# A gated scan and a dense layer on one core: value and state products of both chunks in one visit, the state added in place, four tiles for the gate's split parts

## The chip, the core and the metric

The kernel runs on one core of one Trainium2 chip. The metric is the device time of one execution in microseconds. A profile is one execution recorded by the hardware profiler; its span runs from the first to the last instruction of the program.

The engines are named as in the profile: PE is TensorE (matmuls), PEld its weight loads, DVE is VectorE, ACT is ScalarE, POOL is GpSimd, SP is SyncE, which here only issues DMAs.

## The reference

```python
# all inputs of the scan: (4, 8, 768, 48): batch, head, time, width
mag = sqrt(a_re**2 + a_im**2)
a = (a_re + 1j * a_im) * minimum(mag, 0.999) / (mag + 1e-6)
S = 0                                          # per batch and head, 48 x 48
for t in range(768):
    S = a[t][:, None] * S + outer(k[t], v[t])
    y[t] = q[t] @ S.real
x = y as (3072, 384)                           # 8 heads x 48 side by side
h = x @ w_in                                   # 384 -> 2048
g = h where h >= 1, 0 where h <= -1, else (h + 1)**2 / 4
out = g @ w_out                                # 2048 -> 384
```

So there are two parts: a linear recurrence with a complex decay for each column of the keys, and a dense layer with a piecewise gate.

## The kernel before, in words

**Units and blocks.** The 4 x 768 tokens are cut into 12 units of 256 tokens, and a unit into two chunks of 128. A batch has three units, called parts 0, 1 and 2; units of two batches take turns. Two units form a block of 512 tokens, and there are six blocks. The dense layer works on blocks, the scan on units.

**The scan without a loop over time.** `gates(u)` (L569) makes, on ScalarE and VectorE, running sums of the logarithm and the angle of the decay, multiplies them into keys and queries as a real and an imaginary part, and moves the results by DMA into tiles `hd`, with the 96 rows of a head side by side. What is left is done by `attend(u)` (L898) with matmuls in fp32:

- `scores(c)` (L979): for the eight heads in two groups of four, keys times queries of a chunk, 128 x 128 each, into a bank of PSUM (`sc`, L989). VectorE multiplies by a triangle on the way out (`am`, L997).
- `transposes(c)` (L924): the keys of a chunk, turned, in two groups of four heads (`tp`, L933); ScalarE copies each group out (`kT`, L939).
- `products(c)` (L950): turned keys times values, the chunk's addition to the state (`dp`, L962). VectorE adds it to the old state, into the other one of two tiles of the batch (`st`, L974).
- `values(c, ...)` (L1011): the output of a chunk, for each pair of heads the state times the queries (`yp`, L1030) and then the masked scores times the values (L1038), gathered in one bank. ScalarE copies it to `xr` (L1050), and after the second chunk six DMAs move rows within `xr` (L1062).

`values` and `products` use 64 columns of the array at a time, with two heads side by side; the other matmuls use 96 or 128.

**Banks.** From the third unit on all these outputs take turns over three banks of PSUM, `at0` to `at2`, in the order in which the Python code makes the tiles (`bank`, L917). The other five hold two tiles of gate inputs (`h0`, `h1`) and three of outputs (`o0` to `o2`).

**The dense layer.** `moe(blk)` (L1145) splits x into a high and a low part (fp32r), and does each product in three matmuls. For each of 16 slices f of 128 columns: `gemm1(f)`, nine matmuls in groups of three (`h`, L1160); the gate, on ScalarE and VectorE (`s` L1185, `g` L1204 and L1212, or for the first `SPARE` blocks two more passes on ScalarE, L1195 and L1199, in place of L1212); its split into a high part by a ScalarE cast (`gh`, L1218) and a low one by VectorE (`gl`, L1222); and `gemm2(f)`, nine matmuls in groups of three (`o`, L1235). `gh` and `gl` take turns over six tiles, so three slices can be under way.

**What sets the order.** The code first lists all operations with an estimated cost, what they read and write, and for some a due time. `Plan.order` (L169) then plays them through engine by engine: an engine that is free takes, of the operations that are ready, the one with the earliest due time. The program is emitted in that order, and each engine runs its own list in order on the chip. Three details matter:

- What a tile has to wait for is worked out from the tile that was *made* before it on the same slot, and from those of its operations that are listed already (L155 and L156).
- Parts of a *visit* are glued (L1077): when one is placed, the next is placed right behind it, if all that it waits for has been placed by then (L271); if not, it is taken up later like any other. A gate or output group of three matmuls can then come between.
- An attention visit's due time lies in a window of the block before (`WINDOW`, `EARLY`), spread evenly over the unit's visits (L1109).

The planner's estimates, in ns: PE to another engine 260, ScalarE or VectorE to another 190 (`LAT`); a ScalarE copy from PSUM 80 + 0.77 a column, a VectorE operation 66 + 1.04 a column; `products` 8 x 124, times 0.92 in a visit.

A unit's visits before: scores of chunk 0; transposes of chunk 0; values and products of chunk 0 with half the scores of chunk 1; the other half with the transposes of chunk 1; values and products of chunk 1. In part 2 the last transposes and products fall away.

**Start and end.** Until about 70 us units 0 and 1 and the weights are prepared; PE runs filler matmuls (`idle`, L1290) in the gaps. After the last block some checks of the inputs' ranges follow.

Of the kernel before, what the change touches and what calls it, by code (L numbers as in the profile page):

```python
# [10 lines left out]
F32 = mybir.dt.float32  # L11
# [7 lines left out]
P = 128  # L19
NB = 4  # L20
NH = 8
# [23 lines left out]
LATER = 4  # L45
SUM = 1.0e6
# [18 lines left out]
LATE_MOVE = 1000  # L65
# [7 lines left out]
QUEUE = (2, 0.0)  # L73
WINDOW = (0.0, 0.7)
EARLY = (0.15, 1.05)
HEAD = ((15000, 8000), (8000, 2000))
HOME = 4
SPARE = 2
# [243 lines left out]
def gated_scan_moe(  # L322
# [11 lines left out]
    sums = const.tile([P, 2, P], F32, name="sums")  # L334
    mask = sums[:, 0]
    make_upper_triangular(nc, mask)
    nc.gpsimd.memset(sums[:, 1], 1.0)
# [9 lines left out]
    keys = [const.tile([P, 4 * HR + 32], F32, name=f"kT{g}") for g in range(2)]  # L347
# [32 lines left out]
    def turn_of(tag, n):  # L380
        k = seen.get(tag, 0)
        seen[tag] = k + 1
        return f"{tag}{k % n}"
# [514 lines left out]
    def attend(u):  # L898
# [25 lines left out]
        def transposes(c):  # L924
            cs = slice(c * CH, (c + 1) * CH)
            out = []
            for g in range(2):
                TP = bank([P, 4, HR], f"tp_{u}_{g}_{c}")
                KT = pl.tile(f"kT{g}", lambda g=g: keys[g])

                def run(g=g, TP=TP):
                    for i, h in enumerate(GROUPS[g]):
                        PE_.transpose(TP.get()[:, i, :], head(h)[:, 0, cs], ident[:HR, :HR])  # L933

                def tail(TP=TP, KT=KT):
                    pl.op(
                        "ACT",
                        act(4 * HR, psum=True),
                        lambda: A_.copy(  # L939
                            KT.get()[:, : 4 * HR].rearrange("p (h r) -> p h r", h=4), TP.get()  # L940
                        ),
                        r=[TP],
                        w=[KT],
                    )

                out.append((4 * 83, run, [hd[h // 3] for h in GROUPS[g]], TP, tail))
                carry.setdefault("kT", []).append(KT)
            return out

        def products(c):  # L950
            kT = carry.pop("kT")
            DP = bank([P, NH, D], f"dp_{u}_{c}")
            V_c = carry["V"]
            old = carry.get(b)
            ST = tl(turn_of(f"st{b % 2}", 2), [HR, NH, D], F32, f"st_{u}_{c}")
            carry[b] = ST

            def run():
                for i in range(NH):
                    for a in (0, 64):  # L960
                        k = HR * (i % 4) + a
                        PE_.matmul(  # L962
                            DP.get()[a : a + 64, i, :],
                            kT[i // 4].get()[:, k : k + 64],
                            V_c[0].get()[:, V_c[1], i * D : (i + 1) * D],
                            start=True,
                            stop=True,
                        )

            def tail():  # L970
                if old is None:
                    fn = lambda: V_.tensor_copy(ST.get(), DP.get()[:HR])
                else:
                    fn = lambda: V_.tensor_tensor(ST.get(), old.get(), DP.get()[:HR], op=ALU.add)  # L974
                pl.op("DVE", dve(DM), fn, r=[DP] + ([old] if old else []), w=[ST])

            return [(NH * 124, run, [*kT, V_c[0]], DP, tail)]
# [33 lines left out]
        def values(c, ams, st):  # L1011
# [5 lines left out]
            def part(prs):  # L1017
                Y = bank([P, len(prs), CH], f"yp_{u}_{c}_{prs[0]}")

                def run():  # L1020
                    for i, pr in enumerate(prs):
                        for kind in (0, 1):
                            if kind == 0 and st is None:
                                continue
                            for e in range(2):
# [3 lines left out]
                                if kind == 0:  # L1029
# [4 lines left out]
                                        start=True,  # L1034
                                        stop=False,
                                    )
                                else:
# [4 lines left out]
                                        start=st is None,  # L1042
                                        stop=True,
# [16 lines left out]
                return ((4 if st else 2) * len(prs) * 110 + (400 if prs[0] == 0 else 0), run, r, Y, tail)  # L1060
# [29 lines left out]
        if part == 0:  # L1090
            carry.pop("kT", None)
        state_after = lambda c: part * NC + c < S // CH - 1
        for c in range(NC):
# [9 lines left out]
            pending = (ams, carry.get(b))  # L1103
            carry["V"] = (V, c)
        last = values(NC - 1, *pending)
        if state_after(NC - 1):
            last = last + products(NC - 1)
        visit(last)
# [36 lines left out]
    def moe(blk):  # L1145
# [7 lines left out]
        def gemm1(f):  # L1153
# [25 lines left out]
            GH = tl(turn_of("gg", 6), [P, T], F32R, f"gh_{blk}_{f}")  # L1179
            GL = tl(turn_of("gg", 6), [P, T], F32R, f"gl_{blk}_{f}")  # L1180
# [399 lines left out]
```

## Time and profile before

| | us |
|---|---|
| median of three runs | 577.53 (577.27 to 579.56) |
| the profiled execution | 577.35 |
| its span | 575.6 |
| first gate matmul (`h`) | 70.41 |
| last output matmuls (`o`) begin, 27 in a row | 562.16 |
| PE busy in the span | 561.4 |
| DVE busy | 434.5 |
| ACT busy | 406.1 |
| mean granted clock of TensorE | 0.998 |

In the rows below, `L989` is a line of the kernel, `sc<-hd` is what is written and what is read, and `x8` counts instructions; one matmul in fp32 is two of them, but for transposes. In a timeline a row is a stretch of like instructions: its start, its length, engine, line, and in brackets how long the engine stood idle before it and what it waited for. A group's row gives the busy time, the mean in ns of one, and the idle time before them.

### The profile page before, as it was taken

Reading aid. Unit: us, or ns where it says so; the run is one execution under the profiler, and the core shown is the slowest. Engines: PE = TensorE matmul, PEld = TensorE weight load, DVE = VectorE, ACT = ScalarE, POOL = GpSimd, SP = SyncE. Lnnn points to the kernel's source line nnn. Section 1 sums busy time; section 2 is a strip of 40 time slices with the busy share of each in tenths; the row PEclk is TensorE's granted clock in tenths of the full one; section 3 lists DMA queues with packets and bytes.
Section 4 is the critical chain, followed back from the end, with each engine's and each line's share of the span. In section 5 each row is a group of like instructions: output and inputs, shape, how many; then the busy total and the mean of one; then the engine's idle time right before and its main releaser. Section 6 shows DMA issues by size and latency. Waiting matters only on the chain.

```text
span 575.6 us, 9984 instructions
## 1 busy us (share of the span) xinstructions
PE 561.4 (98%) x3922; PEld 478.4 (83%) x3922; DVE 434.5 (75%) x625; ACT 406.1 (71%) x654; POOL 1.7 (0%) x20
## 2 busy tenths in 40 slices
PE   8999999999999999999999999999999999999995
PEld 7798978888888888888888888888888888888883
DVE  4999999999979498579589878887885544455452
ACT  7776799887998998975576666667643333369972
POOL 1000000000000000000000000000000000000000
PEclk9999999999999999999999999999999999999999
DMA  8676571773641614712601613402312200078811
GB/s 352 250 198 192 163 262 55 192 282 114 188 173 48 195 68 125 237 57 82 174 2 52 202 56 102 153 2 85 114 56 72 74 1 7 21 265 309 298 42 61
DMA packets 23527, 77.42 MB, mean 134 GB/s; under 512 B 4528, under 2 KB 10288, under 8 KB 23472
## 3 DMA queue, kind: packets, MB, share of 16 engines
q1 hardware_dynamic: 23472, 76.70, 40.8%
q8 instruction: 33, 0.54, 0.4%
q14 instruction: 22, 0.18, 0.1%
HBM read 51.90 MB, written 4.72 MB: 98 GB/s over the span
## 4 chain that ended last, share of the span: by engine, by line
PE 78%; DVE 12%; ACT 5%; DMA 2%; issue 1%; SPq 0%; ACTq 0%; DVEq 0%
PE o L1235 30%; PE h L1160 29%; PE sc L989 6%; PE yp L1038 3%; PE yp L1030 3%; PE dp L962 2%; PE tp L933 1%; PE idle L1290 1%; ACT ai L608 1%; DVE kq L725 1%; DMA xr<-xr 1%; DMA ai<-in_art_dram 1%; DVE g L1204 1%; ACT x L608 1%; DVE raw_i L440 1%
## 5 line engine op out<-in xcount | busy, mean ns | idle before, releaser
L1160 PE MATMUL h<-xH,wi 128*128 128x512 f32 x576 | 180.6, 395 | 1.2 <-DVE g L1204 0.9
L1235 PE MATMUL o<-gh,wo 128*128 128x512 f32 x576 | 180.4, 394 | 0.0
L1160 PEld LDWEIGHTS h<-xH,wi 128*128 128x128 f32 x576 | 106.2, 188 | 22.6 <-DVE g L1204 1.1
L1235 PEld LDWEIGHTS o<-gh,wo 128*128 128x128 f32 x576 | 106.3, 188 | 21.6 <-issue 0.7
L1204 DVE TENSOR_TENSOR g<-h,s 128x512 f32<-128x512 f32 x96 | 65.9, 687 | 63.1 <-ACT s L1185 45.6
L1160 PE MATMUL h<-xL,wi 128*128 128x512 f32 x288 | 112.6, 391 | 0.0
L1235 PE MATMUL o<-gl,wo 128*128 128x512 f32 x288 | 112.5, 391 | 0.0
L1185 ACT ACTIVATE s<-h,cst 128x512 f32<-128x512 f32 x96 | 65.7, 685 | 42.0 <-PE h L1160 38.9
L1218 ACT CAST gh<-g 128x512 fp32r<-128x512 f32 x96 | 59.1, 616 | 46.0 <-DVE g L1212 43.6
L1222 DVE TENSOR_TENSOR gl<-g,gh 128x512 fp32r<-128x512 f32 x96 | 66.0, 687 | 31.9 <-ACT gh L1218 31.8
L1160 PEld LDWEIGHTS h<-xL,wi 128*128 128x128 f32 x288 | 54.1, 188 | 12.1 <-DVE xL L1137 0.4
L1235 PEld LDWEIGHTS o<-gl,wo 128*128 128x128 f32 x288 | 54.1, 188 | 11.6
L608 ACT ACTIVATE ai<-ai 128x768 f32<-128x768 f32 x49 | 41.2, 843 | 19.1 <-DVE ai L777 8.6
L989 PE MATMUL sc<-hd 96*128 96x128 f32 x384 | 49.6, 278 | 0.0
L989 PEld LDWEIGHTS sc<-hd 96*128 96x128 f32 x384 | 47.0, 192 | 2.2
L1212 DVE SCALAR_TENSOR_TENSOR g<-s,g 128x512 f32<-128x512 f32 x64 | 44.2, 691 | 1.8
L1038 PE MATMUL yp<-am,V 128*64 128x128 f32 x384 | 35.5, 273 | 0.2 <-DVE am L997 0.2
L997 DVE TENSOR_TENSOR am<-sc,sums 128x512 f32<-128x512 f32 x48 | 32.5, 683 | 3.1 <-PE sc L989 2.8
L1290 PE MATMUL idle<-sums,ident 128*128 128x128 f32 x238 | 31.3, 291 | 1.7 <-POOL sums masks.py:66 1.7
L1030 PE MATMUL yp<-hd,st 96*64 96x128 f32 x320 | 32.1, 278 | 0.3 <-DVE am L997 0.3
L1290 PEld LDWEIGHTS idle<-sums,ident 128*128 128x128 f32 x238 | 30.3, 206 | 2.5 <-POOL sums masks.py:66 1.7
L402 ACT ACT_TABLE_LOAD x21 | 26.9, 1283 | 0.4
(104 smaller groups left out, 651.6 us busy)
## 6 DMA issues: line engine op xcount, KB each, us to landing
chk<-in_wl_dram SPq DMA_DIRECT2D x16, 768.0 KB, 5.2
kq<-in_kq_dram SPq DMA_DIRECT2D x12, 768.0 KB, 4.7
ai<-in_ari_dram SPq DMA_DIRECT2D x10, 768.0 KB, 6.1
hd<-x SPq DMA_DIRECT2D x24, 288.0 KB, 4.1
hd<-kq SPq DMA_DIRECT2D x24, 288.0 KB, 4.9
raw_i<-in_wl_dram SPq DMA_DIRECT2D x8, 768.0 KB, 4.6
raw_o<-in_wl_dram SPq DMA_DIRECT2D x8, 768.0 KB, 5.8
V<-in_v_dram SPq DMA_DIRECT2D x12, 384.0 KB, 3.2
```

The costliest lines, as they stand in the source:

```text
L608: lambda: A_.activation(out(), src(), f, **kw),
L989: PE_.matmul(SC.get()[:, i, :], t[:, 0, cs], t[:, 1, cs], start=True, stop=True)
L1030: PE_.matmul(o_, st.get().rearrange("p h e -> p (h e)")[:, lo : lo + 64], head(h)[:, 1, cs], start=True, stop=False,)
L1038: PE_.matmul(o_, V.get()[:, c, lo : lo + 64], ams[pr // 2].get()[:, 2 * (pr % 2) + e, :], start=st is None, stop=True,)
L1160: PE_.matmul(H.get(), weight["i", f // 2].get()[:, f % 2, part, sl], x.get()[:, j, :], start=j == 0 and n == 0, stop=j == NJ - 1 and n == 2,)
L1185: lambda: A_.activation(SS.get(), H.get(), AF.Relu, bias=c_half, scale=-0.5 if spare else 0.5),
L1204: lambda: V_.tensor_tensor(G.get(), H.get(), SS.get(), op=ALU.max),
L1212: lambda: V_.scalar_tensor_tensor(G.get(), SS.get(), 1.0, G.get(), op0=ALU.min, op1=ALU.mult),
L1218: pl.op("ACT", act(T), lambda: A_.copy(GH.get(), G.get()), r=[G], w=[GH])
L1222: lambda: V_.tensor_tensor(GL.get(), G.get(), GH.get().bitcast(F32), op=ALU.subtract),
L1235: PE_.matmul(PO[m].get(), weight["o", f // 2].get()[:, f % 2, part, sl], g.get(), start=f == 0 and n == 0, stop=f == NF - 1 and n == 2,)
L1290: PE_.matmul(idle["h1"], ident, mask, start=True, stop=True)
```

## The change

It has these parts:

- From unit 2 on (`JOINED`) a unit's visits are: scores of chunk 0 with half of its transposes; the other half with the scores of chunk 1; the transposes of chunk 1; values and products of both chunks. In the last visit the products of chunk 1 stand ahead of the values of chunk 1, and their addition to the state is listed after the values. The tiles of both chunks' scores and transposes are made before any visit is listed.
- For that, two more tiles of masked scores (`am2`, `am3`) and two more of turned keys (`kT2`, `kT3`).
- The state of a batch is one tile, and the products are added in place. For each pair of heads the masked scores' product now comes ahead of the state's.
- `gh` and `gl` take turns over four tiles, and the code lists `gemm2` one slice after `gemm1` where it listed it three after; due times are the same.
- The triangle for the running sums lies in the space of `am3` and is made apart from the mask.
- `SPARE` goes from 2 to 1: the second block's gate uses the VectorE operation (L1212). `HOME`, `WINDOW`, `EARLY`, `QUEUE` and `LATE_MOVE` change: which tiles the first weights land in, the windows of the visits, when SyncE holds back a DMA for a more urgent one, and 1000 ns of allowance for a move that falls away.

```diff
+JOINED = 2
-LATE_MOVE = 1000
+LATE_MOVE = 0
-QUEUE = (2, 0.0)
-WINDOW = (0.0, 0.7)
-EARLY = (0.15, 1.05)
+QUEUE = (2, 10000.0)
+WINDOW = (0.3, 0.7)
+EARLY = (0.6, 0.7)
-HOME = 4
-SPARE = 2
+HOME = 6
+SPARE = 1
...
-    sums = const.tile([P, 2, P], F32, name="sums")
-    mask = sums[:, 0]
+    mask = const.tile([P, P], F32, name="mask")
     make_upper_triangular(nc, mask)
+    sums = sb.tile([P, 4, CH], F32, tag="am3", name="sums", bufs=1)[:, :2]
+    make_upper_triangular(nc, sums[:, 0])
...
-                KT = pl.tile(f"kT{g}", lambda g=g: keys[g])
+                k = g + 2 * (c % 2 if u >= JOINED else 0)
+                KT = pl.tile(f"kT{k}", lambda k=k: keys[k])
...
-            old = carry.get(b)
-            ST = tl(turn_of(f"st{b % 2}", 2), [HR, NH, D], F32, f"st_{u}_{c}")
-            carry[b] = ST
+            first = b not in carry
+            if first:
+                carry[b] = tl(f"st{b % 2}", [HR, NH, D], F32, f"st_{b}")
+            ST = carry[b]
...
-                    fn = lambda: V_.tensor_tensor(ST.get(), old.get(), DP.get()[:HR], op=ALU.add)
+                    fn = lambda: V_.tensor_tensor(ST.get(), ST.get(), DP.get()[:HR], op=ALU.add)
...
-                AM = tl(f"am{g}", [P, 4, CH], F32, f"am_{u}_{g}_{c}")
+                k = g + 2 * c if u >= JOINED else g
+                AM = tl(f"am{k}", [P, 4, CH], F32, f"am_{u}_{g}_{c}")
...
-                        for kind in (0, 1):
+                        for kind in (1, 0):
...
+        if u >= JOINED:
+            (sc0, am0), (sc1, am1) = scores(0), scores(1)
+            tp0 = transposes(0)
+            tp1 = transposes(1) if state_after(1) else []
+            visit(sc0 + tp0[:1])
+            visit(tp0[1:] + sc1)
+            if tp1:
+                visit(tp1)
+            st = state_of()
+            both = values(0, am0, st) + products(0)
+            st = state_of()
+            last = values(1, am1, st, 0)
+            if tp1:
+                ((*dp, add),) = products(1)
+                *head_, (*yp, copy) = last
+                last = [(*dp, lambda: None), *head_, (*yp, lambda: (copy(), add()))]
+            visit(both + last)
+        for c in range(NC) if u < JOINED else ():
...
-            GH = tl(turn_of("gg", 6), [P, T], F32R, f"gh_{blk}_{f}")
-            GL = tl(turn_of("gg", 6), [P, T], F32R, f"gl_{blk}_{f}")
+            GH = tl(turn_of("gg", 4), [P, T], F32R, f"gh_{blk}_{f}")
+            GL = tl(turn_of("gg", 4), [P, T], F32R, f"gl_{blk}_{f}")
...
-        for k in range(NF + LAG):
+        for k in range(NF + 1):
             if k < NF:
                 gemm1(k)
-            if k >= LAG:
-                gemm2(k - LAG)
+            if k:
+                gemm2(k - 1)
```

More of the change, by code (lines that the diff above doesn't have):

```diff
@@ L345, in gated_scan_moe @@
     ones = c_one
-    keys = [const.tile([P, 4 * HR + 32], F32, name=f"kT{g}") for g in range(2)]
+    keys = [const.tile([P, 4 * HR + 32], F32, name=f"kT{g}") for g in range(4)]
     for t in keys:
@@ L946, in transposes @@
                 out.append((4 * 83, run, [hd[h // 3] for h in GROUPS[g]], TP, tail))
-                carry.setdefault("kT", []).append(KT)
+                carry.setdefault(("kT", c), []).append(KT)
             return out
         def products(c):
-            kT = carry.pop("kT")
+            kT = carry.pop(("kT", c))
             DP = bank([P, NH, D], f"dp_{u}_{c}")
-            V_c = carry["V"]
-            old = carry.get(b)
-            ST = tl(turn_of(f"st{b % 2}", 2), [HR, NH, D], F32, f"st_{u}_{c}")
-            carry[b] = ST
+            first = b not in carry
+            if first:
+                carry[b] = tl(f"st{b % 2}", [HR, NH, D], F32, f"st_{b}")
+            ST = carry[b]
             def run():
@@ L964, in run @@
                             kT[i // 4].get()[:, k : k + 64],
-                            V_c[0].get()[:, V_c[1], i * D : (i + 1) * D],
+                            V.get()[:, c, i * D : (i + 1) * D],
                             start=True,
@@ L970, in tail @@
             def tail():
-                if old is None:
+                if first:
                     fn = lambda: V_.tensor_copy(ST.get(), DP.get()[:HR])
                 else:
-                    fn = lambda: V_.tensor_tensor(ST.get(), old.get(), DP.get()[:HR], op=ALU.add)
-                pl.op("DVE", dve(DM), fn, r=[DP] + ([old] if old else []), w=[ST])
-            return [(NH * 124, run, [*kT, V_c[0]], DP, tail)]
+                    fn = lambda: V_.tensor_tensor(ST.get(), ST.get(), DP.get()[:HR], op=ALU.add)
+                pl.op("DVE", dve(DM), fn, r=[DP], w=[ST])
+            return [(NH * 124, run, [*kT, V], DP, tail)]
         def scores(c):
@@ L1009, in scores, with values @@
             return out, ams
-        def values(c, ams, st):
+        def values(c, ams, st, change=400):
             cs = slice(c * CH, (c + 1) * CH)
@@ L1033, in run @@
                                         head(h)[:, 1, cs],
-                                        start=True,
-                                        stop=False,
+                                        start=False,
+                                        stop=True,
                                     )
@@ L1041, in run @@
                                         ams[pr // 2].get()[:, 2 * (pr % 2) + e, :],
-                                        start=st is None,
-                                        stop=True,
+                                        start=True,
+                                        stop=st is None,
                                     )
@@ L1059, in part @@
                 r = [*ams, V, *hd] + ([st] if st else [])
-                return ((4 if st else 2) * len(prs) * 110 + (400 if prs[0] == 0 else 0), run, r, Y, tail)
+                return ((4 if st else 2) * len(prs) * 110 + (change if prs[0] == 0 else 0), run, r, Y, tail)
             def move(j, e):
@@ L1089, in attend @@
         pending = None
-        if part == 0:
-            carry.pop("kT", None)
         state_after = lambda c: part * NC + c < S // CH - 1
-        for c in range(NC):
+        state_of = lambda: carry.get(b)
+        if u >= JOINED:
[16 more added lines that the diff above has]
+        for c in range(NC) if u < JOINED else ():
             before = [] if pending is None else values(c - 1, *pending) + products(c - 1)
@@ L1102, in attend @@
                 visit(tp)
[L1103 to L1108, printed above, removed]
+            pending = (ams, state_of())
+        if u < JOINED:
+            last = values(NC - 1, *pending)
+            if state_after(NC - 1):
+                last = last + products(NC - 1)
+            visit(last)
         for n, i in visits:
```

## The prediction

> **What bounds the kernel now.** I read the page first, for which engine is full and where; then the busy times by stretch; then the timeline of TensorE (PE), for what one step costs and where it waits. The page:
>
> ```profile
> span 575.6 us, 9984 instructions
> PE 561.4 (98%) x3922; PEld 478.4 (83%) x3922; DVE 434.5 (75%) x625; ACT 406.1 (71%) x654; POOL 1.7 (0%) x20
> PE 78%; DVE 12%; ACT 5%; DMA 2%; issue 1%; SPq 0%; ACTq 0%; DVEq 0%
> ```
>
> PE fills 98% of the span and 78% of the chain that ended last. The stretches are the blocks as they run (core, length, then busy us of PE, weight loads, DVE, ACT, POOL, the granted clock, the DMA share and rate):
>
> ```profile
> 82.00:157.00 75.00, 74.69 (x579) 63.66 (x578) 73.89 (x102) 66.89 (x106) 0.00 (x0) 1.00 0.52 167
> 157.00:242.00 85.00, 85.00 (x565) 71.70 (x564) 63.02 (x92) 80.33 (x132) 0.00 (x0) 1.00 0.44 137
> 327.00:412.00 85.00, 85.00 (x625) 72.16 (x624) 70.94 (x103) 55.01 (x85) 0.00 (x0) 1.00 0.28 89
> ```
>
> From 82 us on PE has no hole worth the name (74.69 of 75, then 85.00 of 85); the first block also fills DVE (73.89 of 75) and the second ACT (80.33 of 85). A busy PE can still stretch, so the chain of waits has to show its pace:
>
> ```profile
> 511.16 2.04 PE h L1160 x9
> 513.20 2.04 PE o L1235 x9
> ```
>
> Nine 512-column matmuls take 2.04 us, 0.227 each, with nothing between the groups; a group of three, the planner's unit, takes 0.68. So after 82 us the time is the sum of PE's steps: whatever makes PE stand still there is added in full, and what shortens its queue is gained in full.
>
> **Two value visits made one.** The value and state products use 64 columns of the array, and PE pays when it changes over:
>
> ```profile
> 223.38 0.61 PE L1160 MATMUL h<-xH,wi 128*128 128x512 f32 x2
> 223.83 0.39 PE L1160 MATMUL h<-xL,wi 128*128 128x512 f32 x1
> 224.15 0.44 PE L1030 MATMUL yp<-hd,st 96*64 96x128 f32 x4
> 224.42 0.39 PE L1038 MATMUL yp<-am,V 128*64 128x128 f32 x4
> 224.64 0.39 PE L1030 MATMUL yp<-hd,st 96*64 96x128 f32 x4
> ...
> 225.74 0.39 PE L1038 MATMUL yp<-am,V 128*64 128x128 f32 x4
> 226.06 0.73 PE L1235 MATMUL o<-gh,wo 128*128 128x512 f32 x2
> 226.63 0.39 PE L1235 MATMUL o<-gl,wo 128*128 128x512 f32 x1
> ```
>
> From start to start: into the visit 224.15 - 223.83 = 0.32 for 0.227 (+0.09), the first four 0.27 for 0.22 (+0.05); out of it 0.32 for 0.22 (+0.10), and the next two wide matmuls 0.57 for 223.83 - 223.38 = 0.45 (+0.12). One visit costs 0.36 us in changes. A unit has two, so joining saves 0.36 for each of units 2 to 11: 3.6 us, if the order that the planner makes holds the visit together.
>
> I think that it doesn't. A glued part follows at once only when nothing that it waits for is still unplaced (L271); otherwise PE takes a gate or output group that is ready, and with PE full one nearly always is. With the planner's own numbers: the state products of the first chunk end 0.92 x 8 x 124 = 913 after the values. The second chunk's state products write the bank that the values used, three banks back, so they wait for ScalarE's copy: 260 + (80 + 512 x 0.77) + 190 = 924, later than 913. In a block's second unit they come four banks back, on the first chunk's state products' own bank, and wait for the state's add: 260 + 466 + 190 = 916 behind its matmuls. In a batch's last units the second values wait for that same add. So each joined visit gets one or two groups of three in its middle and is two visits again: 0 gained, 3.6 us if I am wrong. That the add is now in place adds no more than this wait; it is behind the first values in PE's order anyway.
>
> **Scores and transposes in one visit: the wait that I price highest.** The three banks are handed out in the order in which tiles are made: scores of chunk 0, scores of chunk 1, transposes of chunk 0, of chunk 1. Visit two runs the second half of chunk 0's transposes (tile 5), then chunk 1's first scores (tile 2). 5 and 2 are the same bank. The planner sees a tile's predecessor by making order, so it knows no wait here, and forces the scores right behind the transposes. On the chip those scores can't write until ScalarE has copied the transposes out. PE is in order: all its queue stands behind them. A unit of the head shows such a wait, on DVE's reading of scores, and how fast PE starts after its release:
>
> ```profile
> 42.95 0.49 PE L933 MATMUL tp<-ident,hd 96*128 96x96 f32 x4
> 43.53 0.68 DVE L997 TENSOR_TENSOR am<-sc,sums 128x512 f32<-128x512 f32 x1
> 44.27 0.55 PE L933 MATMUL tp<-ident,hd 96*128 96x96 f32 x4 [0.82 <-DVE am L997]
> ```
>
> The multiply ends at 44.21, PE starts 0.06 later. How soon the copy of transposes comes (first ScalarE's waits for transposes, total, times and longest, then the group of copies, then single visits):
>
> ```profile
> ACT kT L939 <- PE tp L933: 7.4, 10, 1.7
> L939 ACT COPY kT<-tp 128x384 f32<-128x384 f32 x40 | 17.3, 478 | 7.4 <-PE tp L933 7.4
> 80.50 0.82 PE L933 MATMUL tp<-ident,hd 96*128 96x96 f32 x8
> 83.64 0.85 ACT L939 COPY kT<-tp 128x384 f32<-128x384 f32 x2
> 124.37 0.82 PE L933 MATMUL tp<-ident,hd 96*128 96x96 f32 x8
> 125.52 0.85 ACT L939 COPY kT<-tp 128x384 f32<-128x384 f32 x2
> 204.82 0.82 PE L933 MATMUL tp<-ident,hd 96*128 96x96 f32 x8
> 205.71 0.47 ACT L939 COPY kT<-tp 128x384 f32<-128x384 f32 x1
> 334.41 0.82 PE L933 MATMUL tp<-ident,hd 96*128 96x96 f32 x8
> 334.94 0.86 ACT L939 COPY kT<-tp 128x384 f32<-128x384 f32 x2 [0.36 <-PE tp L933]
> 335.01 0.70 PE L1160 MATMUL h<-xH,wi 128*128 128x512 f32 x2
> 335.56 0.40 PE L1160 MATMUL h<-xL,wi 128*128 128x512 f32 x1
> ```
>
> Eight transposes take 0.82, four (42.95) 0.49, so four more cost 0.33, the time after which the scores would start without a wait. With ScalarE idle (334.41) the first copy starts 0.53 after the transposes did and takes 0.48; with 0.06 the scores start at 1.07: a stall of 0.74. At 204.82 the copy starts at 0.89: 1.10. In the first block, 124.37: 1.15, so 1.36; 80.50: 3.14, so 3.35. These are the nearest rows: same tiles, same engine, only who waits is new. Ten times ScalarE stood waiting for transposes; the 40 copies go in pairs, so that is about half the visits. So I take the middle of 0.74 and 1.10, 0.92, for the eight units outside the first block, 7.4, and 1.36 for the two in it, 2.7: **10 us**. The lowest is ten times 0.74 = 7.4, the highest 8 x 1.10 + 2 x 3.35 = 15.5. A gain is excluded: the copy can't start before the transposes end.
>
> In visit one the transposes' first half takes the bank of the second scores as well, but this the planner knows, and it puts output groups between. Such a border costs little: transposes to gate 335.01 - 334.41 = 0.60 for 8 x 0.08, then 0.55 for 0.45: 0.06 or less in all, 0.6 us for ten units, within the margin below. I take nothing.
>
> **Four tiles for the gate's split parts.** A cast may now start only when the output products of two gates before are done, not three. The narrowest place I found is in block 4:
>
> ```profile
> 467.61 0.62 ACT L1218 CAST gh<-g 128x512 fp32r<-128x512 f32 x1 [1.48 <-DVE g L1212]
> 470.95 0.39 PE L1235 MATMUL o<-gl,wo 128*128 128x512 f32 x1
> 478.38 2.08 PE o L1235 x9
> ```
>
> The cast at 467.61 (gate 9) would wait for gate 7's last product, at 470.95, and be some 3.6 us later; its own products come at 478.38 or just before, against 467.61 + 3.6 + 0.62 + 0.69 for cast and rest = 472.5. PE waits for nothing: 0, since the planner knows this wait and puts other ScalarE work ahead of it. If that cover were gone the cast's queue would stand 3.6 us and still end in time.
>
> **Second block's gate on DVE.** Sixteen multiplies are added:
>
> ```profile
> L1212 DVE SCALAR_TENSOR_TENSOR g<-s,g 128x512 f32<-128x512 f32 x64 | 44.2, 691 | 1.8
> ```
>
> 16 x 0.69 = 11 us onto 63.02 of 85, and two ScalarE passes a gate come off 80.33. DVE then has 74 of 85, about what it had beside full PE in block 3 (70.94). 0 on PE; it shortens ScalarE's queue for units 4 and 5, for which 0.92 above allows.
>
> **What only moves the order.** Six weights in place of four at the start pick the same four tiles (4 and 5 fall on xH1, xL1 either way): 0. A second triangle and two more pads are a few of GpSimd's 1.7 us, behind the mask that PE's first matmul needs: 0. The windows, the DMA's allowance and SyncE's holding back shift what is taken when. Their gain is bounded by the waits of PE that they could remove:
>
> ```profile
> 70.41 0.73 PE L1160 MATMUL h<-xH,wi 128*128 128x512 f32 x2 [0.26 <-ACT xH L1130]
> 77.64 0.73 PE L1160 MATMUL h<-xH,wi 128*128 128x512 f32 x2 [0.93 <-DVE g L1204]
> 128.93 0.44 PE L1030 MATMUL yp<-hd,st 96*64 96x128 f32 x4 [0.26 <-DVE am L997]
> ```
>
> 1.45 us; I allow as much the other way and take 0. No hd, V or weight transfer is added or passes another queue.
>
> **Sum.** The profiled execution took 577.35 us (575.6 of span, 1.75 around it), 0.18 under the median of 577.53. 577.35 + 0 (joined visit) + 10.1 (stalls) + 0 = 587.4. Own range: 577.35 + 7.4 - 1.45 = 583.3 to 577.35 + 15.5 + 1.45 = 594.3.
>
> **Rivals.**
> *The visit joins and no stall comes* (faster). The place is the second visit: were a group or two of the gate (0.68 each) put between transposes and scores, or the copy done by another way of handing out banks, 1.07 would be covered and the 3.6 us of changes gained: 577.35 - 3.6 = 573.8, 572.3 to 575.2. It decides for faster once more than 2.9 us of net saving is left, that is with stalls under 0.07 us a unit. For it: the visits are glued to hold together, and 913 against 924 is close. Against: banks 2 and 5. 0.13.
> *The change does nothing that PE sees*: no stall, and the visit split as reckoned: 577.4, 575.9 to 578.8. 0.10.
> *Stalls, but the visit holds*: 577.35 + 10.1 - 3.6 = 583.9, 579.7 to 587. 0.12.
> *PE has room that its busy time hides*: stalls of 1 us a unit are made good, 577.4 again. In the trace PE's pace inside the blocks is 2.04 us for nine without a break, so there is nothing to catch up with. 0.04. [...]
> *The first block comes apart*: DVE is full there, a late mask multiply holds transposes in visit one as well, over 594.3. 0.04.
> Forecast: 0.57.
>
> **Numbers.** Over or under 0.5% (2.9 us) is about what a measurement of this kernel can tell from no change, so faster ends at 574.6 and slower begins at 580.4. Faster 0.13 (first rival). Same 0.15: the second and fourth, 0.14, and 0.01 from the low end of the third. Slower 0.72. The range runs from the second rival's lower end to near the forecast's upper one, 575.5 to 593.5; it leaves out the first rival and the last, 0.17. The cases with stalls hold 0.73; the likeliest one's own range is 583.3 to 594.3.
>
> **What would show it.** Ten holes of 0.7 us and more before the score matmuls, put down to ScalarE's copy of kT, eight to twelve us in all, none of them from 500 us on; two runs of 64-column matmuls a unit with one or two groups of three between; stretches of 85 us grown to about 87; nothing put down to the casts. Wrong if score matmuls follow transposes without a hole, if value and state products of both chunks stand in one unbroken run, or if gate matmuls start to wait for the split parts.

## The result, and the profile after

| | before | after |
|---|---|---|
| median, us | 578.54 (577.27 to 580.79), 4 runs | 602.44 (601.61 to 603.5), 4 runs |
| ratio, with 95% interval | | 1.041 (1.0369 to 1.045) |
| the profiled execution, us | 577.35 | 602.24 |
| its span, us | 575.6 | 600.4 |
| mean granted clock | 0.998 | 0.984 |

The change makes the kernel 4.1% slower. The direction was as predicted; the size was not: 10 us were forecast, 24 came, and 602 lies above the range's end of 593.5.

The page of after: the span, the busy times, and the granted clock in 40 slices of 15 us.

```profile
span 600.4 us, 10064 instructions
PE 571.7 (95%) x3912; PEld 484.6 (81%) x3912; DVE 444.0 (74%) x641; ACT 390.6 (65%) x622; POOL 2.2 (0%) x24
PEclk9999989999989999988999999999999999999999
```

PE is busy for 95% of a longer span, and the clock row has four places under 9. The waits of after name two kinds of holes, before the scores and before the gate's matmuls (total us, times, longest):

```profile
PE sc L993 <- ACT kT L942: 12.5, 10, 2.4
PE h L1181 <- DVE g L1225: 3.9, 4, 1.5
```

The stretches of after, in the columns that the prediction explained (the third number from the end is the granted clock):

```profile
82.00:157.00 75.00, 72.22 (x556) 60.91 (x555) 69.50 (x94) 63.35 (x98) 0.00 (x0) 0.98 0.44 144
157.00:242.00 85.00, 80.21 (x526) 67.88 (x525) 65.41 (x98) 55.73 (x88) 0.00 (x0) 0.96 0.37 106
242.00:327.00 85.00, 80.80 (x519) 67.80 (x518) 61.59 (x90) 51.70 (x83) 0.00 (x0) 0.96 0.36 109
327.00:412.00 85.00, 83.03 (x567) 69.91 (x567) 69.51 (x102) 54.01 (x84) 0.00 (x0) 1.00 0.31 96
```

The loss is uneven. Between 157 and 327 us PE lacks 4.8 and 4.2 us of 85 and the clock is at 0.96; from 327 us on it lacks 2 or less and the clock is full. ScalarE, which copies the transposes out, has *less* to do in these four stretches than before, most of all in the second (55.73 of 85 where it had 80.33).

**The priced stall, short and long.** Two units in the timeline of after. The first, with ScalarE idle:

```profile
316.20 0.49 PE L936 MATMUL tp<-ident,hd 96*128 96x96 f32 x4
316.73 0.48 ACT L942 COPY kT<-tp 128x384 f32<-128x384 f32 x1 [0.86 <-PE tp L936]
317.26 2.05 PE L993 MATMUL sc<-hd 96*128 96x128 f32 x16 [0.57 <-ACT kT L942]
```

From the transposes' start to the scores' start it is 1.06 us; without a wait it would be 0.33. So this unit loses 0.73, which is the 0.74 that the prediction had for an idle ScalarE. (The bracket says 0.57, because the last transposes count as busy for 0.16 longer than their step.) The second:

```profile
168.22 0.49 PE L936 MATMUL tp<-ident,hd 96*128 96x96 f32 x4
...
168.84 0.67 ACT L1206 ACTIVATE s<-h,cst 128x512 f32<-128x512 f32 x1
169.41 0.57 ACT L1283 COPY ob<-o 128x512 f32<-128x512 f32 x1
169.88 0.85 ACT L610 ACTIVATE ai<-ai 128x768 f32<-128x768 f32 x1
...
170.62 0.47 ACT L942 COPY kT<-tp 128x384 f32<-128x384 f32 x1
...
171.15 3.60 PE L993 MATMUL sc<-hd 96*128 96x128 f32 x16 [2.44 <-ACT kT L942]
```

Three other pieces of ScalarE's work stand ahead of the copy. The planner doesn't know that PE stands still for this copy, and so the copy has no precedence. All ten waits: 12.5 by the waits, and 10 x 0.16 of drain, 14.1 us.

**Half clock.** The scores at 171.15 take 3.60 us where 16 of them take 1.95. The windows of after show why; here are two stretches with a hole, and then all five stretches of 3.4 us that ran at half the clock:

```profile
168.00:171.40 3.40, 0.96 (x10) 0.78 (x9) 3.37 (x6) 3.40 (x7) 0.00 (x0) 1.00 0.77 271
260.10:263.50 3.40, 1.90 (x16) 1.66 (x15) 1.14 (x2) 1.92 (x4) 0.00 (x0) 1.00 0.44 154
...
86.00:89.40 3.40, 3.40 (x12) 2.85 (x11) 2.76 (x5) 1.99 (x3) 0.00 (x0) 0.51 0.00 0
171.40:174.80 3.40, 3.40 (x17) 3.40 (x17) 0.75 (x3) 3.27 (x7) 0.00 (x0) 0.50 0.08 28
222.60:226.00 3.40, 3.40 (x17) 3.40 (x16) 0.94 (x3) 0.00 (x0) 0.00 (x0) 0.50 0.02 5
263.50:266.90 3.40, 3.40 (x11) 2.52 (x10) 3.25 (x6) 2.94 (x6) 0.00 (x0) 0.50 0.25 82
270.40:273.80 3.40, 3.40 (x16) 3.21 (x16) 1.40 (x3) 0.00 (x0) 0.00 (x0) 0.50 0.00 0
```

Each follows a stretch in which PE was idle for 1.5 to 2.4 us: 1.62, 2.44, 2.02, 1.50 and 2.13, in order of time (the first two rows: 3.40 - 0.96 = 2.44 and 3.40 - 1.90 = 1.50). Four of the five follow waits for the copy; the one at 263.5 follows a wait of gate matmuls for the gate, 1.50 us. PE is full in them by its busy time, 3.40 of 3.40, at a granted clock of 0.50 or 0.51. The timeline of after inside one of them:

```profile
264.15 1.05 PE L1181 MATMUL h<-xH,wi 128*128 128x512 f32 x2
...
265.43 1.05 PE L1181 MATMUL h<-xH,wi 128*128 128x512 f32 x2
```

A group of three takes 265.43 - 264.15 = 1.28 us in place of 0.68. If half of each is lost, five such stretches cost 5 x 3.4 / 2 = 8.5 us, an estimate; the mean clock gives the same, (0.998 - 0.984) x 600 = 8.4.

**The balance.** 14.1 (scores) + 8.5 (half clock) + 3.9 - 0.9 = 3.0 (gate's matmuls, which waited 0.9 before) = 25.6, where the span grew by 24.8. Where the 0.8 between them lies was not traced.

**The joined visit.** The timeline of after, PE alone, at the first unit with the new visits:

```profile
95.18 1.09 PE L965 MATMUL dp<-V,kT 128*64 128x48 f32 x32
96.19 0.73 PE L1256 MATMUL o<-gh,wo 128*128 128x512 f32 x2
...
99.14 1.14 PE L965 MATMUL dp<-V,kT 128*64 128x48 f32 x32
```

Between the state products of the two chunks (`dp`) stand four gate and output groups, from 96.19 to 99.14. So it is in all ten units, with three to five groups between the first chunk's state products and what follows them. The visit is in two parts, as reckoned.

### The profile page after: what moved, and what is told of

It reads as the page before. It is cut to its first block, busy times and chain, and to the rows that moved or that the text cites. A ratio compares the mean times of both kernels' runs of the same rounds, so it can differ in the third digit from the quotient of the medians.

```text
span 600.4 us, 10064 instructions
## 1 busy us (share of the span) xinstructions
PE 571.7 (95%) x3912; PEld 484.6 (81%) x3912; DVE 444.0 (74%) x641; ACT 390.6 (65%) x622; POOL 2.2 (0%) x24
## 4 chain that ended last, share of the span: by engine, by line
PE 68%; DVE 11%; ACT 9%; DMA 7%; issue 2%; SPq 1%; ACTq 0%; DVEq 0%
PE o L1256 26%; PE h L1181 26%; PE sc L993 6%; PE yp L1042 3%; PE dp L965 3%; DMA out_dram<-ob 3%; PE yp L1034 3%; ACT ai L610 2%; DMA hd<-kq 2%; DMA hd<-x 1%; ACT x L610 1%; SPq L394 1%; PE tp L936 1%; ACT s L1206 1%; DVE g L1225 1%
## 5 line engine op out<-in xcount | busy, mean ns | idle before, releaser
L1256 PE MATMUL o<-gh,wo 128*128 128x512 f32 x576 | 182.5, 398 | 0.0
L1181 PEld LDWEIGHTS h<-xH,wi 128*128 128x128 f32 x576 | 107.7, 190 | 26.9 <-DVE g L1225 4.9
L993 PE MATMUL sc<-hd 96*128 96x128 f32 x384 | 53.7, 296 | 12.9 <-ACT kT L942 12.5
L993 PEld LDWEIGHTS sc<-hd 96*128 96x128 f32 x384 | 50.2, 207 | 16.0 <-ACT kT L942 14.4
L1233 DVE SCALAR_TENSOR_TENSOR g<-s,g 128x512 f32<-128x512 f32 x80 | 55.2, 690 | 2.0
L1001 DVE TENSOR_TENSOR am<-sc,mask 128x512 f32<-128x512 f32 x48 | 32.1, 684 | 17.5 <-PE sc L993 17.4
L1311 PE MATMUL idle<-mask,ident 128*128 128x128 f32 x228 | 30.5, 293 | 1.7 <-POOL mask masks.py:66 1.7
L1311 PEld LDWEIGHTS idle<-mask,ident 128*128 128x128 f32 x228 | 29.5, 208 | 2.5 <-POOL mask masks.py:66 1.7
L1054 ACT COPY xr<-yp 128x512 f32<-128x512 f32 (+2 forms) x30 | 14.9, 496 | 19.3 <-PE yp L1034 18.1
```

The costliest lines, as they stand in the source:

```text
L993: PE_.matmul(SC.get()[:, i, :], t[:, 0, cs], t[:, 1, cs], start=True, stop=True)
L1181: PE_.matmul(H.get(), weight["i", f // 2].get()[:, f % 2, part, sl], x.get()[:, j, :], start=j == 0 and n == 0, stop=j == NJ - 1 and n == 2,)
L1233: lambda: V_.scalar_tensor_tensor(G.get(), SS.get(), 1.0, G.get(), op0=ALU.min, op1=ALU.mult),
L1256: PE_.matmul(PO[m].get(), weight["o", f // 2].get()[:, f % 2, part, sl], g.get(), start=f == 0 and n == 0, stop=f == NF - 1 and n == 2,)
L1311: PE_.matmul(idle["h1"], ident, mask, start=True, stop=True)
```

## The experiments

Theory: the unplanned wait for the copy of transposes carries most of the loss, with the half clock that follows its longer holes. Rivals: the new windows, the four tiles, the state in place, or the new packing of scores and transposes carries it.

Each ratio is to runs of the kernel before that were taken alongside; their medians lie between 578.5 and 578.9.

| kernel | median, us | ratio to before (95%) |
|---|---|---|
| after | 602.44 | 1.041 (1.0369 to 1.045) |
| banks in the order of use | 586.60 | 1.0143 (1.009 to 1.0196) |
| the wait told to the planner | 586.82 | 1.0111 (1.0049 to 1.0173) |
| old visits | 585.44 | 1.011 (1.0071 to 1.0149) |
| old visits, six tiles | 587.72 | 1.0164 (1.0132 to 1.0195) |
| old visits, old `WINDOW` | 580.99 | 1.0047 (1.0028 to 1.0066) |
| old visits, old `WINDOW` and `EARLY` | 579.50 | 1.0018 (1.0003 to 1.0034) |
| old visits, all numbers old | 578.05 | 0.9988 (0.9971 to 1.0004) |
| banks in the order of use, all numbers old | 581.81 | 1.0058 (1.0036 to 1.008) |
| the same, value visit in two | 579.80 | 1.003 (1.0013 to 1.0046) |
| the same, value visit held together | 582.59 | 1.0073 (1.0056 to 1.0091) |

### The unplanned wait, taken away in three ways

**Banks in the order of use.** From the kernel after; chunk 0's transposes are made ahead of chunk 1's scores, so that transposes and the scores right behind them lie in different banks:

```diff
-            (sc0, am0), (sc1, am1) = scores(0), scores(1)
+            sc0, am0 = scores(0)
             tp0 = transposes(0)
+            sc1, am1 = scores(1)
```

> The changed kernel, with chunk 0's transposes made ahead of chunk 1's scores, so that banks are handed out in the order of the visits and no transposes stand on the bank of the scores behind them. Theory A (the wait for the copy of transposes carries the whole loss: 14.2 us of waits of score matmuls for ScalarE, 8.2 us because PE's clock is halved for 3.4 us after the long ones, and most of the 3.4 us that gate matmuls wait longer for the gate): no waits of sc for kT, granted clock 0.99 or more, 577 to 580 us. Rival B (four tiles for the split parts and the narrower windows cost by themselves): the waits of h for VectorE's gate stay at some 4.5 us, 580 to 584. Rival C (scores and transposes packed in common visits are bad whatever their banks): 590 or more.

**The wait told to the planner.** From the kernel after; banks as there, but the first part of chunk 1's scores also reads the copied keys, so the planner sees the wait and can put other work into it:

```diff
             visit(sc0 + tp0[:1])
+            copied = carry[("kT", 0)][1]
+            sc1[0] = (*sc1[0][:2], sc1[0][2] + [copied], *sc1[0][3:])
             visit(tp0[1:] + sc1)
```

> The changed kernel with its banks as they are; the scores behind the transposes name the copied keys as something that they read, so the planner knows of the wait and puts gate or output groups between. Theory A says that sharing the bank costs nothing once it is known: 577 to 580 us, no hole of 0.7 us before scores. If sharing itself costs, holes of some 0.3 to 0.7 us stay and it comes out 581 to 590.

**Old visits.** From the kernel after, with everything else of the change:

```diff
-JOINED = 2
+JOINED = 12
```

> The changed kernel with the old visits for all units: the four tiles, the state in place, the second block's gate on VectorE and the new windows stay. Theory A: 576 to 579 us, since these parts cost nothing on PE. Rival B: 580 or more, with h waiting for the gate for over 3 us in all and casts waiting for output products.

All three come out between 585.4 and 586.8, and the 576 to 580 that the theory had expected came in none of them. The first two leave the new visits as they are and are aimed at one wait alone; each is some 15.7 us faster than after. So this wait, with its half clock, is the cause of two thirds of the loss, and it is shown in two independent ways. The waits of the first kernel have no scores left that wait for a copy; those of the second have a tenth. First kernel, then second:

```profile
PE h L1182 <- DVE g L1226: 6.0, 5, 2.3
```

```profile
PE h L1183 <- DVE g L1227: 5.9, 4, 2.6
PE sc L993 <- ACT kT L942: 1.3, 2, 0.7
```

What is left, 7 to 8 us over before, isn't in the visits alone: old visits have it too, and in all three the gate's matmuls wait for the gate, some 6 us. Each of the three also still has one or two stretches at half clock behind holes (mean granted clock 0.991, 0.995 and 0.992, against 0.998 in before). The longest of these holes, from the timeline of the kernel with old visits:

```profile
164.80 1.95 PE L993 MATMUL sc<-hd 96*128 96x128 f32 x16
166.58 0.82 PE L936 MATMUL tp<-ident,hd 96*128 96x96 f32 x8
169.19 0.69 ACT L1206 ACTIVATE s<-h,cst 128x512 f32<-128x512 f32 x1 [2.57 <-DMA out_dram<-ob]
170.68 0.73 PE L1181 MATMUL h<-xH,wi 128*128 128x512 f32 x2 [3.27 <-DVE g L1225]
```

and from that of before, at the same place in the program:

```profile
155.30 1.95 PE L989 MATMUL sc<-hd 96*128 96x128 f32 x16
...
168.63 1.09 PE L962 MATMUL dp<-V,kT 128*64 128x48 f32 x32
...
170.56 0.72 PE L1160 MATMUL h<-xH,wi 128*128 128x512 f32 x2
```

This is the border of two blocks. The outputs' copies `ob` use the same tiles in turn as the gate's `s`, so the new block's first gates wait until the outputs have been stored (ScalarE 2.57 us, then PE 3.27). In before attention stands at this border: the unit's scores run at 155.30, its transposes follow between gate and output groups, and from 166.81 to 170.56 values, state products and the next scores run without a hole. With the new windows the unit's first scores come at 164.80 and its values only at 173.82, so PE has nothing left to run.

### Which number does that

All four start from the kernel with old visits.

**All numbers old**: four tiles, the state in place and the order of the value products stay; `WINDOW`, `EARLY`, `QUEUE`, `LATE_MOVE` and `SPARE` as before. (`HOME` keeps its new value here and below.)

```diff
-LATE_MOVE = 0
+LATE_MOVE = 1000
-QUEUE = (2, 10000.0)
-WINDOW = (0.3, 0.7)
-EARLY = (0.6, 0.7)
+QUEUE = (2, 0.0)
+WINDOW = (0.0, 0.7)
+EARLY = (0.15, 1.05)
-SPARE = 1
+SPARE = 2
```

> The changed kernel with the old visits (as in the run with old visits, 585.4 us, where gate matmuls waited 7.6 us for the gate) and with the old WINDOW, EARLY, QUEUE, LATE_MOVE and SPARE; the four tiles and the state in place stay. Theory B1 (the new windows leave PE without attention work at a block's start, where the gate's tiles wait for the output's DMAs): 577 to 579 us, waits of h for the gate about 1 us as before the change. Theory B2 (four tiles hold the gate up): 583 or more, waits of h stay.

**Six tiles**: `gh` and `gl` over six tiles, listed three slices apart as before, new numbers. (The listing, and two tiles of turned keys that the old visits don't use and that fall away, are not in these lines.)

```diff
-            GH = tl(turn_of("gg", 4), [P, T], F32R, f"gh_{blk}_{f}")
-            GL = tl(turn_of("gg", 4), [P, T], F32R, f"gl_{blk}_{f}")
+            GH = tl(turn_of("gg", 6), [P, T], F32R, f"gh_{blk}_{f}")
+            GL = tl(turn_of("gg", 6), [P, T], F32R, f"gl_{blk}_{f}")
```

> The changed kernel with the old visits and with six tiles for the split parts, listed three slices apart as before; the new windows and numbers stay. B1: 583 to 586 us, the waits of h at the blocks' starts stay. B2: 577 to 579.

**Old windows**: `WINDOW` and `EARLY` alone as before.

```diff
-WINDOW = (0.3, 0.7)
-EARLY = (0.6, 0.7)
+WINDOW = (0.0, 0.7)
+EARLY = (0.15, 1.05)
```

> The changed kernel with the old visits and the old WINDOW and EARLY alone; four tiles, QUEUE, LATE_MOVE and SPARE stay new. B1: 577 to 579 us. B2, or a theory that the other numbers matter: 583 or more.

**Old `WINDOW`** alone:

```diff
-WINDOW = (0.3, 0.7)
+WINDOW = (0.0, 0.7)
```

> The changed kernel with the old visits and the old WINDOW alone; EARLY, which sets the windows of the first block's attention only, stays new, as do the other numbers and the four tiles. If what costs is that attention work no longer stands ready when a block starts (the holes at 167, 256 and 514 us of the run with old visits and new windows), these holes go and it comes out 579 to 581 us. If the first block's windows are to blame, the hole at 167 us, at the start of the second block, stays, and 583 or more.

Six tiles are no faster than four: 1.0164 against 1.011, with overlapping intervals, and the gate's matmuls still wait 8.7 us for the gate (583 to 586 us had been expected for this case, 587.72 came). So the four tiles are not the cause. With all numbers old the loss is gone (0.9988, an interval that holds 1), so four tiles, the state in place and the order of the value products cost nothing together. Of the 585.44 - 578.05 = 7.4 us, `WINDOW` carries 4.5 (585.44 to 580.99), `EARLY` 1.5 (to 579.50), and the three other numbers 1.5 together. Only the first step is clear of the noise; the intervals on both sides of each of the other two overlap. The waits follow. With old `WINDOW`, and then with all numbers old:

```profile
PE h L1181 <- ACT ai L610: 1.4, 1, 1.4
```

```profile
PE h L1181 <- DVE g L1225: 0.9, 1, 0.9
PE yp L1042 <- DVE am L1001: 0.5, 2, 0.3
```

With old `WINDOW` one hole of 1.4 us is left at the first border of blocks, beside the 0.9 at the start that before has too; with all numbers old only that 0.9 is left of the gate's waits.

### The new visits with nothing else in the way

**Banks in the order of use, all numbers old**: the first kernel of this section with the five numbers of before, as in the diff above.

> The changed kernel with banks in the order of the visits (586.6 us, no waits for the copy of transposes) and the old WINDOW, EARLY, QUEUE, LATE_MOVE and SPARE; new visits, four tiles. B1: 577 to 580 us, as the joined visit is split and gains nothing. B2: 584 or more. A theory that the new visits cost by themselves: over 581 with no waits of h.

581.81 against 578.05 with old visits and the same numbers: the new visits themselves cost 3.8 us, although their unplanned wait is gone. (The theory that had expected over 581 us for this had expected no waits of `h`; there are some.) The waits of this kernel are spread thin:

```profile
PE h L1182 <- DVE g L1226: 2.1, 3, 1.3
PE yp L1042 <- DVE am L1001: 1.3, 3, 0.6
PE o L1257 <- DVE gl L1244: 1.2, 1, 1.2
```

They sum to 4.6 where old visits have 0.9 + 0.5 = 1.4; that is 3.2 of the 3.8. The likely reason is that half scores and transposes together leave the planner larger pieces and the three banks are taken in a burst; that was not tried on its own.

**Value visit held together, and in two.** From that kernel, scores and transposes have visits of their own, and each chunk's state products stand ahead of its values where both are needed, with the addition to the state listed after the values. In one kernel the planner lets PE take nothing else until the glued part is ready, so the value visit stays whole in the six units where both products are needed; in the other it is two visits.

```diff
+            elif held and not left[held[0]]:
+                i = held.pop()
...
+                    if held and e == "PE":
+                        continue
...
-                visit([dp0, y0, dp1, *y1[:-1], end], hold=True)
+                visit([dp0, y0])
+                visit([dp1, *y1[:-1], end])
```

(The first lines are the holding, the last three the difference between the two.)

> A visit that really holds. Old numbers and windows, four tiles, banks in the order of the visits; scores and transposes of each chunk in visits of their own; the last visit is products 0, values 0, products 1, values 1, and the planner keeps PE for it until its next part can run (in the six units that have products 1; the others keep two visits). If a change into and out of the 64-column matmuls costs 0.36 us as the prediction reckoned, six changes fewer: 2.2 us under the same kernel with the visit in two. If the waits inside the visit (values 1 on the state's add, products 1 on its bank) eat that up, no difference.

> The same kernel with that visit in two (products 0, values 0; products 1, values 1), a gate or output group or more between them. 577 to 580 us, and 2.2 us more than the run in which the visit holds; equal if waits inside that one eat up the gain.

Held together is 2.8 us slower (582.59 and 579.80, intervals 1.0056 to 1.0091 and 1.0013 to 1.0046), where 6 x 0.36 = 2.2 should have been gained. The waits of the held kernel, and one held visit in its timeline:

```profile
PE yp L1051 <- DVE st L986: 2.1, 2, 1.7
PE yp L1051 <- DVE st L984: 1.7, 2, 1.4
```

```profile
140.85 1.09 PE L974 MATMUL dp<-V,kT 128*64 128x48 f32 x32
...
142.43 0.69 DVE L1257 TENSOR_TENSOR gl<-g,gh 128x512 fp32r<-128x512 f32 x1
143.03 0.55 DVE L986 TENSOR_TENSOR st<-st,dp 96x384 f32<-96x384 f32 x1
...
143.64 0.44 PE L1051 MATMUL yp<-am,V 128*64 128x128 f32 x4 [1.70 <-DVE st L986]
```

The second values need the state's add, and VectorE has other work ahead of it, a `gl` among it: PE stands for 1.70 us inside the visit to save 0.36. The waits are 3.8 us together. Between 80 and 560 us PE stands idle for 5.0 us in the held kernel and 1.6 in the one in two; these 3.4 are more than the 3.2 by which the held profile is longer, so hardly anything of the 2.2 shows. That a change into and out of the 64-column matmuls costs 0.36 us is thus not confirmed. What the change was to save was not had in this shape, and the planner's splitting is the cheaper way here.

### How long a hole costs the clock

These two are the kernel before with waits of PE put in. In `transposes` of chunk 0, second group, ScalarE copies the bank out k extra times, and the transposes are then done again, so they wait for the copies.

**Ladder**: k = 1, 1, 1, 2, 2, 3, 3, 4, 4, 5 for units 2 to 11.

```diff
+LADDER = (1, 1, 1, 2, 2, 3, 3, 4, 4, 5)
...
+                    if g == 1 and c == 0 and u >= 2:
+                        for _ in range(LADDER[u - 2]):
+                            A_.copy(
+                                KT.get()[:, : 4 * HR].rearrange("p (h r) -> p h r", h=4),
+                                TP.get(),
+                            )
+                        turn()
```

> The kernel before, with a made wait in ten places: behind the second group of chunk 0's transposes in units 2 to 11, ScalarE copies that group 1, 1, 1, 2, 2, 3, 3, 4, 4, 5 times, and PE does the four transposes again behind these copies. Each copy 0.48 us, so waits of some 0.75, 0.75, 0.75, 1.2, 1.2, 1.7, 1.7, 2.2, 2.2, 2.6 us and 0.33 us for the transposes done twice: 18 us. Theory A (a hole of about 1.5 us and more in PE halves its clock for 3.4 us, which costs 1.7 us): five drops or so behind the last five, none behind those of 1.2 and less: 577.4 + 18 + 8.5 = 604 us. Rival (the drops in the changed kernel come from something else, such as the mix of small matmuls around): no drops, 595 us, granted clock 0.998.

One execution: 602.33 us, with 17.3 us of idle time before the ten repeated transposes, 0.6 to 3.7 us each. The half clock came only twice where five times were expected (mean granted clock 0.990), after the hole of 3.74 us and one of 2.61, and not after one of 2.90 and two of 1.6 and 2.1; so "a hole of 1.5 us or more" doesn't decide. The windows of this kernel, the two after 295.4 with the hole of 2.90 across their border, then the one of 3.74:

```profile
295.40:298.80 3.40, 1.85 (x14) 1.41 (x12) 3.14 (x5) 2.74 (x6) 0.00 (x0) 1.00 0.00 0
298.80:302.20 3.40, 2.06 (x12) 1.75 (x13) 0.78 (x3) 2.98 (x7) 0.00 (x0) 1.00 0.00 0
...
391.00:394.40 3.40, 0.94 (x7) 0.87 (x8) 1.55 (x2) 2.99 (x7) 0.00 (x0) 0.99 0.00 0
394.40:397.80 3.40, 3.40 (x12) 2.27 (x12) 1.56 (x3) 1.61 (x3) 0.00 (x0) 0.50 0.00 0
```

The long hole that was divided over two stretches left 1.85 and 2.06 us of work in them, and the clock stayed at 1.00; 0.94 in one stretch was followed by one at 0.50.

**Small matmuls after**: three copies in units 4 to 11; after them 20 transposes in even units and 4 in odd ones (in units 2 and 3 too, without copies), to see whether what PE does in the rest of the stretch counts.

```diff
+LADDER = (0, 0, 3, 3, 3, 3, 3, 3, 3, 3)
...
+                        for _ in range(5 if u % 2 == 0 else 1):
+                            turn()
```

> The kernel before with a made wait like the ladder's, three copies in each of units 4 to 11, so some 1.6 us (more where ScalarE is busy); in the units with an even number PE does the four transposes five times behind it, 1.65 us, in the others once. Theory (the clock is set by fixed stretches of 3.41 us; over about 2 us without a matmul in one of them halves it for the next, and about 1.5 us is enough where the rest is transposes or scores, not where it is wide matmuls): drops behind most of the even units, none behind odd ones with a wait under 1.9 us. Rival (only the hole counts): as many behind odd as behind even ones, none under 1.9 us.

One execution: 611.52 us, eight holes of 1.59 us (two of them longer, 3.04 and 2.33). Half clock followed in units 5 to 9, and not in 4, 10 and 11 (mean granted clock 0.982). So it isn't even against odd, and neither is it the hole alone, since holes of 1.6 us did both. The windows of units 4 and 5:

```profile
164.80:168.20 3.40, 1.81 (x16) 1.46 (x15) 2.99 (x4) 2.96 (x7) 0.00 (x0) 1.00 0.23 77
168.20:171.70 3.50, 3.50 (x28) 2.83 (x28) 0.17 (x1) 2.64 (x7) 0.00 (x0) 1.00 0.62 200
209.20:212.60 3.40, 1.79 (x16) 1.44 (x15) 2.70 (x5) 3.02 (x7) 0.00 (x0) 1.00 0.00 0
212.60:216.00 3.40, 3.40 (x9) 2.17 (x7) 2.40 (x5) 2.10 (x4) 0.00 (x0) 0.50 0.01 2
```

1.81 us of work kept the clock, 1.79 lost it, and in after even 1.90 lost it (260.1 to 263.5). So between 1.79 and 1.90 us the amount of work alone didn't decide, and what did was not found.

## Why the prediction was right and where it was wrong

The forecast had 10.1 us of stalls and nothing else; the span grew by 24.8. Of the 14.7 between, by the trace of after, 8.5 are the half clock, 4.0 the stalls' size and 3.0 the longer waits for the gate, less the 0.8 that was not traced.

- **"whatever makes PE stand still there is added in full"**: right as a lower bound. 14.1 us of stalls and 3.0 of longer waits came in full, and the half clock on top. The rival by which PE has room that its busy time hides is refuted: in the first two kernels without the copy's wait, 15.7 us came back for the 14.1 of stalls and part of the half clock.
- **The step that failed by most: a hole is priced at its own length.** The half clock behind the holes, 8.5 us, has no term in the sum. Nothing in the trace of before showed it after 82 us, where it has no hole over 0.3 us; the clock of 0.998 was read as given, and what a hole does to the work behind it was not asked. Even with the upper bound of the stalls the forecast's own range ended at 594.3.
- **The stall on the copy, 10 us**: right in mechanism, place and number (ten waits, the last of them ahead of 500 us), too low in size: 14.1. The step that was mis-sized is "0.92 for the eight units outside the first block", 7.4 in all, which measured 11.0 (worked out for each unit as for the two shown: 0.73 three times, 0.76, 1.02, 2.18, 2.29, 2.60); the first block's two measured 1.32 and 1.78, 3.1 for 2.7. That 14.1 lies inside the bounds of 7.4 and 15.5 is luck: the eight are over their upper bound of 8.8, and the two far under theirs of 6.7. The 0.92 was read from two copies of before, which start 0.53 and 0.89 after their transposes; what counts is what the planner puts ahead of a copy of which it doesn't know that PE waits. The unit at 168 us lost 2.6 us in a stretch where ScalarE is busy for 55.73 of 85.
- **Also failed: "What only moves the order", "1.45 us; I allow as much the other way and take 0."** The waits that exist bound a gain, but they don't bound a loss. Windows and the other numbers cost 7.4 us with old visits and 4.8 with new ones (586.60 to 581.81), because the border of blocks lost the attention work that covered it. The 3.0 of gate waits in after and the 1.7 of half clock behind one of them fit the 4.8. The prediction looked at what the windows could remove, and not at which holes attention was filling.
- **The visit is split, 0 gained**: right in the trace of after, with three to five groups in the middle where one or two were reckoned. The 3.6 us that it would have gained in the first rival were not found: held together in six units it lost 2.8 us, since the values wait on VectorE's add. That rival, and the third, counted only the changes saved.
- **Scores and transposes in common visits, "I take nothing"**: with the wait gone and all numbers old, the new visits cost 3.8 us. Why was not settled.
- **Four tiles, state in place, order of the value products, 0**: right (0.9988, 0.9971 to 1.0004, together). In that kernel ScalarE's casts wait 15.6 us for output products, which they don't in before, and PE loses nothing by it, as reckoned.

The shares in the medians: 15.8 the unplanned wait with its half clock, 4.8 the numbers, 3.8 the new visits, 0 the rest, together the 24.4 between 602.44 and 578.05. They are steps of one path and not independent: the 7.4 against 4.8 shows it. Whether the unplanned wait would have been as dear with the old windows was not tried. No kernel here beats the one before.

## What to carry to other kernels

Before two pieces of work that write the same memory bank are put back to back, look at which queue empties the bank between them; if whatever orders that queue doesn't know that somebody waits, the price is not the copy's 0.74 us but everything that is queued ahead of it (here 0.73 to 2.60 us a unit). When a schedule's windows are moved, don't ask only which waits they could remove: look for the places, such as borders of blocks, that the moved work was covering. And a stall of TensorE cost more than its length here: in after, each of the three stretches of 3.4 us that were left with 2.0 us or more of idle time (2.02, 2.13 and 2.44) was followed by one at half clock, by estimate up to 3.4 / 2 = 1.7 us on top; at 1.5 to 1.6 us of idle time this came in some places and not in others.

## What was not expected of the hardware

In after the granted clock falls to 0.50 or 0.51 five times, for 3.4 us each time. These stretches begin at 86.0, 171.4, 222.6, 263.5 and 270.4 us, and the differences are 25, 15, 12 and 2 times 3.41, to within 0.2 us. (In the kernel with banks in the order of use the clock stayed at 0.50 from 253.4 to 260.2 us, two such stretches in a row.)

The length of the hole alone doesn't order what was seen; the idle time of PE inside one such stretch does so better. In the ladder 2.90 us divided over two stretches (1.55 and 1.34) left the clock at 1.00 in both, and 2.46 us in one (391.0 to 394.4) were followed by 0.50. In after, from 80 us to the last output matmuls and divided at the same multiples of 3.41 us, the stretches with 2.44 (168.0 to 171.4), 2.13 (267.0 to 270.4), 2.02, 1.62 and 1.50 us of idle time were followed by 0.50 or 0.51, and all others, of which the emptiest had 1.16 us (127.0 to 130.4), by 1.00. Between these it went either way: with small matmuls after, 1.61 us (209.2 to 212.6) were followed by 0.50 and 1.59 us (164.8 to 168.2) by 1.00. What decides there was not found. A stretch doesn't have to be empty: those of after had 0.96 us, and even 1.90 us, of matmuls in them.
